# Sliding-window attention and MLP on one core: q and k in DRAM by 48 rows a head, values' halves swapped at the store, addends and divisions placed away from their transfers

## The chip, the cores and the metric

One core of a Trainium2 chip runs the whole program. Its engines each work through their own instructions in order: PE (TensorE, matmuls), PEld (the weight loads of TensorE), DVE (VectorE), ACT (ScalarE), POOL (GpSimd) and SP (SyncE), which here only issues transfers. SBUF is the on-chip working memory, PSUM the memory into which TensorE writes, DRAM the memory outside. The metric is device microseconds of one execution; the profile's span runs from the first to the last instruction of one profiled execution.

## The reference

```python
def _A_ref(x, wqkv, wo):                     # S=2048, D=512, H=32 heads of 16, window W=256
    q, k, v = split(x @ wqkv)
    scores = einsum("bhqd,bhkd->bhqk", q, k) * Dh ** -0.5
    mask = (i - j >= 0) & (i - j < W)
    p = softmax(where(mask, scores, -1e9))
    return merge_heads(einsum("bhqk,bhkd->bhqd", p, v)) @ wo
def _B_ref(x, w1, b1, w2, b2):               # F=1792
    return gelu(x @ w1 + b1) @ w2 + b2
g = sigmoid((x * gate_w).sum(-1, keepdims=True))
return g * A + (1 - g) * B
```

All arrays are float32. The kernel computes a dense product as three matmuls of a rounded high part and a low rest (`mm3`, lines L90 to L92), to keep precision with the narrower matmul type.

## The kernel before

The 2048 tokens are four pieces `t` of 512, and a piece is four blocks of 128. TensorE's work is one long dense program and, woven into it, attention:

- `qkv(t)` transposes x, computes q, k and v, splits q and k into high and low parts (ScalarE L248, VectorE L251) and stores them in DRAM: `SQ`, `SK` (L252), `SV` (L273). The stage lasts some 158 us; attention begins within its last quarter.
- `mlp(n)` runs the two halves of the MLP over the four pieces in eight turns. The end of a block, `y_end` (L647), adds an addend `ya`: the bias `b2` in the first half, the sum of the first half (`YA`) in the second.
- `final(t)` multiplies the attention output with `wo`, scales it by the gate and adds the MLP's part `yb` (L710).

Attention goes over 8 groups of 4 heads, and in each over 16 blocks of 128 keys. `att_max` (matmul L404, VectorE L409) finds row maxima, 8 blocks ahead of `att_exp` (matmul L445, ScalarE L460, GpSimd L451 and L454), which uses them; `att_pv` (L486) multiplies with the values and, by an extra column of ones, gives the denominators. For these, q and k lie in SBUF as 48 rows a head: in `ks` high, low, high, and in `qs` low, high, high, so that one matmul gives the three products. For every group and chunk of 512 tokens, `att_load` and `att_load_v` fetch k, q and v from DRAM. In DRAM a head has 32 rows (high and low), so a tile of 48 takes two loads, one of 32 rows and one of 16; the second head of a pair lies 64 keys displaced in `ks`, and its rows go in two pieces (L365, L367). For the values, the two halves of a block change places (partitions 0 to 63 and 64 to 127) for two of the four heads, at the load (L390, L392).

When a group pair is done for a chunk, `nd` (numerators and denominators) is stored in `ND` (L509). `att_norm` then loads the denominators `den` (L527) and numerators `num` (L530), takes the reciprocal (L533), stores it in `RD` (L534), reads it back spread over 16 rows as `rb` (L535), multiplies (L538) and stores the result in `OT` (L539). `load_o` fetches that as `or` (L567) and splits it into `ot` (L570, L573) for `final`.

The order on PE, ACT, DVE and POOL is written by the program: each function calls `tick` with an assumed duration, and `after(ns, fn)` puts a follow-up that many assumed nanoseconds later (`LAND` 10500, `LANDO` 4500, `NORM` 4500). The order of SP's transfers is made by the scheduling layer from the same program. SP issues them one after another; each waits for its data, for its buffer, and for the transfer eight places earlier in the queue, whose semaphore it uses again. Most of what the change touches is in these lines:

```python
# before, att_norm: what sets the division's place
nc.sync.dma_start(den, v[:, 16, :].rearrange("i (j c) -> i j c", c=32))
nc.sync.dma_start(num, v[:, 0:16, :])
after(NORM, rcp), after(3 * NORM, mul)
# before, mlp, y_start: the addend is loaded when its block's matmuls start
nc.sync.dma_start(ya, b2.partition_broadcast(128))
```

Of the kernel before, what the change touches and what calls it, by code (L numbers as in the profile page):

```python
# [32 lines left out]
def gated_mix(ctx: ExitStack, tc: tile.TileContext, x, wqkv, wo, w1, b1, w2, b2, gate_w, out):  # L33
# [18 lines left out]
    SQ = [dr.tile([H, 16, 2, T], F32, name=f"SQ{t}") for t in range(NT)]  # L52
    SK = [dr.tile([H, 16, 2, T], F32, name=f"SK{t}") for t in range(NT)]
# [180 lines left out]
    def qkv_qk(t, j):  # L234

        xt = xts[t]
        dst, i = (SQ[t], j) if j < NC else (SK[t], j - NC)
# [12 lines left out]
        def lo():  # L250
            nc.vector.tensor_sub(e[:, 1 - h], p, f32(e[:, h]))  # L251
            nc.sync.dma_start(dst[8 * i:8 * i + 8].rearrange("h d s c -> (h d) s c"), f32(e))  # L252
            done.add(("qk", t, j))
        after(100, hi), after(700, lo)

    def qkv_v(t, b):
# [91 lines left out]
    def load_stack(src, high, put):  # L348

        put(0, src.rearrange("h d s c -> (d s) h c"))  # L350
        put(32, src[:, :, high].rearrange("h d c -> d h c"))

    def load_k(g_, c, prs):

        need(("qk", c, NC + g_ // 2))
        for pr in range(prs.start, prs.stop):
            v = f32(ks[:, pr, 2 * c * T:2 * (c + 1) * T])

            def put_a(r, src):
                dst = v[r:r + src.shape[0]].rearrange("r (n x) -> r n x", x=256)[:, :, 64:192]  # L360
                nc.sync.dma_start(dst, src[:, 0].rearrange("r (n x) -> r n x", x=128))

            def put_b(r, src):
                w = v[48 + r:48 + r + src.shape[0]]
                nc.sync.dma_start(w[:, 192:960].rearrange("r (n x) -> r n x", x=256)[:, :, 0:128],  # L365
                                  src[:, 0, 64:448].rearrange("r (n x) -> r n x", x=128))
                nc.sync.dma_start(w.rearrange("r (n x) -> r n x", x=64)[:, 0:16:15],  # L367
                                  src[:, 0].rearrange("r (n x) -> r n x", x=64)[:, 0:8:7])
            for s, put in enumerate((put_a, put_b)):
                h = 4 * g_ + 2 * pr + s  # L370
                load_stack(SK[c][h:h + 1], 0, put)

    def att_load(g_, c, q_only=False):
        need(("qk", c, g_ // 2))
        cs = slice(c * T, (c + 1) * T)
        if not q_only:
            load_k(g_, c, slice(0, 2))
        for s in range(2):
            heads = slice(4 * g_ + s, 4 * g_ + 3 + s, 2)

            def put(r, src):
                nc.sync.dma_start(f32(qs[48 * s + r:48 * s + r + src.shape[0], :, cs]), src)
            load_stack(SQ[c][heads], 1, put)

    def att_load_v(g_, c):
# [4 lines left out]
        nc.sync.dma_start(dst[:, :, 34:68], src[:, :, 68 * g_ + 34:68 * g_ + 68])  # L390
        for r in (0, 64):
            nc.sync.dma_start(dst[64 - r:128 - r, :, 0:34], src[r:r + 64, :, 68 * g_:68 * g_ + 34])  # L392
# [130 lines left out]
    def att_norm(t, c):  # L523
# [4 lines left out]
        num = sb.tile([128, T], F32, tag="tmp", bufs=3, name=f"num{t}_{c}")  # L528
        rb = sb.tile([128, T], F32, tag="tmp", bufs=3, name=f"rb{t}_{c}")
        nc.sync.dma_start(num, v[:, 0:16, :])  # L530

        def rcp():
            nc.vector.reciprocal(den, den)  # L533
            nc.sync.dma_start(RD[t][c].rearrange("h (j c) -> (h j) c", c=32), den)  # L534
            nc.sync.dma_start(rb, RD[t][c].unsqueeze(1).broadcast_to([8, 16, T]))  # L535

        def mul():
            nc.vector.tensor_mul(num, num, rb)  # L538
# [13 lines left out]
    def load_o(t):  # L552

        if t % 2 == 0:
            v = sb.tile([128, NC, 2, T], F32R, tag="xt", bufs=1, name=f"ot{t}")
            ot = [v[:, c] for c in range(NC)]
        else:
            ot = [sb.tile([128, 2, T], F32R, tag="h", bufs=8, name=f"ot{t}_{c}") for c in range(NC)]
        xts["o", t] = ot
        for c in range(NC):  # L560
# [11 lines left out]
            def lo(c=c, raw=raw):  # L572
                nc.vector.tensor_sub(ot[c][:, 1], raw, f32(ot[c][:, 0]))  # L573
                done.add(("ot", t, c))
            land = LAND if t == 0 else LANDO
            after(land + 700 * c, hi), after(land + 700 * c + 600, lo)
# [29 lines left out]

    def mlp(n):
        half, t = TURNS[n]
        last = n % NT == NT - 1
# [20 lines left out]
        ps_, yas = {}, {}  # L630

        def y_start(b):
            if n + 1 == len(TURNS) and b == 2:
                load_o(0)
            ps_[b] = ps.tile([128, D], F32, tag="d", bufs=2, name=f"y{t}_{half}{b}")
            ya = sb.tile([128, D], F32, tag="ya", bufs=2, name=f"ya{t}_{half}{b}")
            if half == 0:
                nc.sync.dma_start(ya, b2.partition_broadcast(128))
            else:
                need(("y", 0, t, b))  # L640
                nc.sync.dma_start(ya, YA[t][slice(b * 128, (b + 1) * 128)])
            yas[b] = ya

        def y_end(b):
            ts = slice(b * 128, (b + 1) * 128)
            y = sb.tile([128, D], F32, tag="sq", bufs=2, name=f"yo{t}_{half}{b}")
            nc.vector.scalar_tensor_tensor(y, ps_[b], 0.5, yas[b], op0=ALU.mult, op1=ALU.add)  # L647
# [172 lines left out]
```

## Time and profile before

| | |
|---|---|
| median of 3 runs | 793.07 us (791.7 to 795.51) |
| the profiled execution | 797.43 us, span 795.7 us |
| granted TensorE clock, mean | 0.987 |
| busy: PE, DVE, ACT, POOL | 760.4, 532.7, 433.1, 386.8 us |
| transfers | 138.74 MB on SP's queue, 57.4% of 16 transfer engines over the span |
| stages by the timeline | projections to 158 us, attention and MLP to about 740, last projection to the end |

In the rows of the profile a group or timeline row names line, engine, instruction, output and inputs with their shapes; a bracket gives the idle time of the engine ahead of it and what ended it. A row of waits gives the total, the number of times and the longest, in us. A row of the windows view gives a stretch, its length, each engine's busy time with its instructions in brackets, and then three numbers: the granted TensorE clock, the busy share of the 16 transfer engines, and GB/s.

### The profile page before, as it was taken

The page shows a single profiled execution, that of the slowest core. Times are in us where ns is not written, and L with a number is a line of the kernel's source. Part 1 is how long each engine was busy: PE and PEld are TensorE (multiplying, and loading weights), DVE is VectorE, ACT ScalarE, POOL GpSimd, SP SyncE. Part 2 cuts the span into 40 slices and gives each one's busy share as a digit, 9 for nine tenths or more (in the row PEclk, how much of TensorE's full clock was granted, in tenths as well). Part 3 has the DMA queues.
Part 4 walks back from the last instruction along what each step waited for, and adds up shares of the span by engine and source line. Part 5 has one row for each costly group of instructions (what it writes and reads, how often), then busy time and mean ns, then how long its engine had stood idle before and what let it go on. Part 6 is the DMA issues. An engine that isn't in the chain of part 4 may idle for free. (4 is left out here: it accounts for less than half of the span.)

```text
span 795.7 us, 18550 instructions
## 1 busy us (share of the span) xinstructions
PE 760.4 (96%) x6102; PEld 629.9 (79%) x6102; DVE 532.7 (67%) x1548; ACT 433.1 (54%) x945; POOL 386.8 (49%) x1125
## 2 busy tenths in 40 slices
PE   8999999989899999999999799999989999999878
PEld 6888888867788878788878677888868788878766
DVE  4433233889579758867996598679757876892433
ACT  4434433466368437745874476458626754875340
POOL 2200000047557755765576467658745775777000
PEclk9999999999999999999999999999989999999999
DMA  9985856536645554755345646534654465546872
GB/s 295 353 301 200 305 176 215 205 106 226 156 113 122 189 161 112 216 141 146 104 116 171 172 137 211 142 86 102 207 155 133 127 206 146 127 143 197 259 258 93
DMA packets 139984, 139.93 MB, mean 176 GB/s; under 512 B 60016, under 2 KB 93040, under 8 KB 139888
## 3 DMA queue, kind: packets, MB, share of 16 engines
q1 hardware_dynamic: 139888, 138.74, 57.4%
q8 instruction: 49, 0.80, 0.5%
q14 instruction: 47, 0.39, 0.2%
HBM read 83.63 MB, written 55.05 MB: 174 GB/s over the span
## 5 line engine op out<-in xcount | busy, mean ns | idle before, releaser
L409 DVE CUSTOM_DVE_ANT_0 jm<-sm,mask 128x384 bf16<-128x384 f32 (+2 forms) x512 | 269.5, 526 | 62.5 <-PE sm L404 34.0
L460 ACT ACTIVATE pt<-st 128x320 f32<-128x320 f32 (+4 forms) x512 | 206.9, 422 | 150.3 <-PE st L445 144.2
L451 POOL TENSOR_SCALAR_AFFINE_SELECT pt<-pt 64x128 f32<-64x128 f32 x512 | 177.3, 346 | 202.5 <-ACT pt L460 182.3
L404 PE MATMUL sm<-ks,qs 96*128 96x384 f32 (+2 forms) x512 | 172.5, 340 | 20.6 <-DVE M L409 19.1
L445 PE MATMUL st<-qs,ks 104*128 104x320 f32 (+4 forms) x512 | 156.3, 307 | 0.7 <-ACT pt L460 0.7
L454 POOL TENSOR_SCALAR_AFFINE_SELECT pt<-pt 64x128 f32<-64x128 f32 x448 | 155.8, 348 | 0.0
L404 PEld LDWEIGHTS sm<-ks,qs 96*128 96x128 f32 x512 | 96.9, 189 | 54.4 <-DVE M L409 32.6
L445 PEld LDWEIGHTS st<-qs,ks 104*128 104x128 f32 x512 | 97.9, 191 | 18.7 <-ACT pt L460 1.1
L90 PE MATMUL y<-w,h 128*128 128x512 f32 x224 | 91.6, 409 | 0.0
L91 PE MATMUL y<-w,h 128*128 128x512 f32 x224 | 88.7, 396 | 0.0
L92 PE MATMUL y<-w,h 128*128 128x512 f32 x224 | 88.3, 394 | 0.0
L429 POOL CAST qs<-tt 8x256 fp32r<-8x256 f32 x128 | 61.5, 481 | 49.7 <-PE u L92 39.1
L90 PE MATMUL u<-mx,w 128*128 128x512 f32 x196 | 81.7, 417 | 0.0
L91 PE MATMUL u<-mx,w 128*128 128x512 f32 x196 | 77.9, 397 | 0.0
L92 PE MATMUL u<-mx,w 128*128 128x512 f32 x196 | 77.6, 396 | 0.0
L486 PE MATMUL pv_st<-pt,vbuf 64*32 64x320 f32 (+4 forms) x1408 | 76.7, 358 | 0.0
L486 PE MATMUL pv_sm<-pt,vbuf 64*32 64x320 f32 (+4 forms) x1408 | 76.2, 358 | 0.5 <-DVE M L409 0.5
L486 PEld LDWEIGHTS pv_st<-pt,vbuf 64*32 64x32 f32 x1408 | 58.4, 109 | 5.8 <-issue 0.9
L486 PEld LDWEIGHTS pv_sm<-pt,vbuf 64*32 64x32 f32 x1408 | 55.9, 109 | 8.7 <-DVE M L409 2.5
L251 DVE TENSOR_TENSOR qke<-qk,qke 128x512 fp32r<-128x512 f32 x32 | 22.1, 690 | 48.9 <-ACT qke L248 40.5
L92 PEld LDWEIGHTS y<-w,h 128*128 128x128 f32 x224 | 42.2, 188 | 10.5
L248 ACT ACTIVATE qke<-qk 128x512 fp32r<-128x512 f32 x32 | 19.1, 598 | 55.9 <-PE qk L92 37.0
(123 smaller groups left out, 1316.9 us busy)
## 6 DMA issues: line engine op xcount, KB each, us to landing
mx<-XT SPq DMA_DIRECT2D x24, 512.0 KB
SQ<-qke SPq DMA_DIRECT2D x16, 512.0 KB
SK<-qke SPq DMA_DIRECT2D x16, 512.0 KB
qs<-SQ SPq DMA_DIRECT2D x64, 128.0 KB
ND<-nd SPq DMA_DIRECT2D x32, 256.0 KB
raw_w<-in_B_w_dram SPq DMA_DIRECT2D x28, 256.0 KB
SV<-vx SPq DMA_DIRECT2D x16, 272.0 KB
xr<-in_A_x_dram SPq DMA_DIRECT2D x16, 256.0 KB
```

The lines of the kernel that those rows point to most:

```text
L90: nc.tensor.matmul(p, lh, rh, start=first, stop=False)
L91: nc.tensor.matmul(p, lh, rl, start=False, stop=False)
L92: nc.tensor.matmul(p, ll, rh, start=False, stop=last)
L251: nc.vector.tensor_sub(e[:, 1 - h], p, f32(e[:, h]))
L404: nc.tensor.matmul(p[:, :w], qs[0:96, pr, b * 128:(b + 1) * 128], of_head(ks[0:96, pr, 2 * k0:2 * (k0 + w)], s), start=True, stop=True)
L409: nc.vector.tensor_tensor_reduce(junk[:, :w], p[:, :w], mask[:, 384 - w:384], 1.0, -3e38, ALU.add, ALU.max, M[:, b % RB, i:i + 1])
L429: nc.gpsimd.tensor_copy(dst, tt[32 * i:32 * i + 8].unsqueeze(1).broadcast_to([8, 2, RB, 32]))
L445: nc.tensor.matmul(p[:, :w], ks[0:104, pr, 2 * k0:2 * k0 + 128], qs[0:104, pr, k0:k0 + w], start=True, stop=True)
L451: nc.gpsimd.affine_select(out=v[:, :, 0:64], in_=v[:, :, 0:64], pattern=[[0, 2], [1, 64]], compare_op=ALU.is_ge, fill=0.0, base=0, channel ...
L454: nc.gpsimd.affine_select(out=v[:, :, W:W + 64], in_=v[:, :, W:W + 64], pattern=[[0, 2], [-1, 64]], compare_op=ALU.is_ge, fill=0.0, base=- ...
L460: nc.scalar.activation(pt[:, pr, :w], p[:, :w], AF.Exp, scale=SCALE)
L486: nc.tensor.matmul(pv[r // 64][32 * i:32 * i + 32, q - c * T:e - c * T], vs(i, r), rhs(r), start=start, stop=last, skip_group_check=True, ...
```

## The change

- `SQ` and `SK` have 48 rows a head. After a q or k tile, two transfers are issued: high and low (two of three rows), and once more the row that occurs twice. A chunk's q is then one load for all four heads, k one load a head. `SK` is one tensor over all tokens, so that the displaced head is loaded across the chunk's border: the last 64 keys of a chunk come with the next chunk's load.
- The values' halves change places when they are stored: three transfers a block instead of one. The load of a chunk is then one transfer.
- `att_norm`: `den` is loaded as before, the reciprocal comes 6000 ns behind (4500 before); `num` and `rb` are requested at 10500 and multiplied at 17000 (13500 before).
- The addend `ya` of a block is loaded when the block two before it has ended (`ya_load`).
- `load_y(0)` goes ahead to the last MLP block, `load_o(t + 1)` ahead of the remaining `load_y`; the last piece's last part is loaded by itself in the third block of `final(2)`. `LANDO` is 5000 instead of 4500.

```diff
-    SQ = [dr.tile([H, 16, 2, T], F32, name=f"SQ{t}") for t in range(NT)]
-    SK = [dr.tile([H, 16, 2, T], F32, name=f"SK{t}") for t in range(NT)]
+    SQ = [dr.tile([H, 48, T], F32, name=f"SQ{t}") for t in range(NT)]
+    SK = dr.tile([H, 48, S], F32, name="SK")
...
-            nc.sync.dma_start(dst[8 * i:8 * i + 8].rearrange("h d s c -> (h d) s c"), f32(e))
+            to = dst[8 * i:8 * i + 8].rearrange("h (d u) c -> (h d) u c", u=3)
+            nc.sync.dma_start(to[:, 0:2], f32(e))
+            nc.sync.dma_start(to[:, 2], f32(e[:, h]))
...
-            nc.sync.dma_start(SV[t][ts], vx)
+            to = SV[t][ts].rearrange("p (g s a) c -> p g s (a c)", s=2, a=2)
+            vy = vx.rearrange("p (g s a) c -> p g s (a c)", s=2, a=2)
+            nc.sync.dma_start(to[:, :, 1], vy[:, :, 1])
+            for r in (0, 64):
+                nc.sync.dma_start(to[64 - r:128 - r, :, 0], vy[r:r + 64, :, 0])
...
-            for s, put in enumerate((put_a, put_b)):
-                h = 4 * g_ + 2 * pr + s
-                load_stack(SK[c][h:h + 1], 0, put)
+            for s in range(2):
+                src = SK[4 * g_ + 2 * pr + s]
+                v = f32(ks[48 * s:48 * s + 48, pr])
+                if s == 0:
+                    w = f32(ks[0:48, pr, 2 * c * T:2 * (c + 1) * T]).rearrange("r (n x) -> r n x", x=256)
+                    nc.sync.dma_start(w[:, :, 64:192], src[:, c * T:(c + 1) * T].rearrange("r (n x) -> r n x", x=128))
+                    continue
+                k0, n = (c * T - 64, NB) if c else (64, NB - 1)
+                w = v[:, 2 * k0 + 64:2 * k0 + 64 + 256 * n].rearrange("r (n x) -> r n x", x=256)
+                nc.sync.dma_start(w[:, :, 0:128], src[:, k0:k0 + 128 * n].rearrange("r (n x) -> r n x", x=128))
...
-        for s in range(2):
-            heads = slice(4 * g_ + s, 4 * g_ + 3 + s, 2)
...
-            load_stack(SQ[c][heads], 1, put)
+        nc.sync.dma_start(f32(qs[0:96, :, c * T:(c + 1) * T]),
+                          SQ[c][4 * g_:4 * g_ + 4].rearrange("(a s) r c -> (s r) a c", a=2))
...
-        nc.sync.dma_start(dst[:, :, 34:68], src[:, :, 68 * g_ + 34:68 * g_ + 68])
-        for r in (0, 64):
-            nc.sync.dma_start(dst[64 - r:128 - r, :, 0:34], src[r:r + 64, :, 68 * g_:68 * g_ + 34])
+        nc.sync.dma_start(dst, src[:, :, 68 * g_:68 * g_ + 68])
...
-        nc.sync.dma_start(num, v[:, 0:16, :])
...
-            nc.sync.dma_start(rb, RD[t][c].unsqueeze(1).broadcast_to([8, 16, T]))
+
+        def back():
+            for name, src in (("num", v[:, 0:16, :]), ("rb", RD[t][c].unsqueeze(1).broadcast_to([8, 16, T]))):
+                tiles.append(sb.tile([128, T], F32, tag="tmp", bufs=3, name=f"{name}{t}_{c}"))
+                nc.sync.dma_start(tiles[-1], src)
...
-        after(NORM, rcp), after(3 * NORM, mul)
+        after(6000, rcp), after(10500, back), after(17000, mul)
...
+    def ya_load(k):
+        n, b = divmod(k, NB)
+        if n == len(TURNS):
+            return
+        half, t = TURNS[n]
+        yas[k] = ya = sb.tile([128, D], F32, tag="ya", bufs=2, name=f"ya{t}_{half}{b}")
+        if half == 0:
+            nc.sync.dma_start(ya, b2.partition_broadcast(128))
+        else:
+            need(("y", 0, t, b))
+            nc.sync.dma_start(ya, YA[t][slice(b * 128, (b + 1) * 128)])
...
-            nc.vector.scalar_tensor_tensor(y, ps_[b], 0.5, yas[b], op0=ALU.mult, op1=ALU.add)
+            nc.vector.scalar_tensor_tensor(y, ps_[b], 0.5, yas.pop(n * NB + b), op0=ALU.mult, op1=ALU.add)
+            ya_load(n * NB + b + 2)
...
+            if n + 1 == len(TURNS) and b == 3:
+                load_y(0)
...
-        if t == 0:
-            for i in (0, 1, 2):
-                load_y(i)
-        if t == 1:
-            load_y(3)
         if t < NT - 1:
-            load_o(t + 1)
+            load_o(t + 1, range(NC) if t < NT - 2 else range(NC - 1))
+        for i in ((1, 2), (3,), (), ())[t]:
+            load_y(i)
...
+            if t == NT - 2 and b == 2:
+                load_o(t + 1, range(NC - 1, NC))
...
-LANDO = 4500.0
+LANDO = 5000.0
```

PE's and POOL's instructions stand in the same order as before. Three places show what moves on the others.

On SP, in the middle of attention, from the store of the third chunk's `nd` of the second group pair to the load of its denominators (`raw_w` are MLP weights, `OT` a finished division, `YA` a sum of the first MLP half). Before:

```order
L509 DMA ND_1_99<-nd_2_6192 128x512
L365 DMA ks<-SK_76 32x3x128
L367 DMA ks<-SK_76 32x2x64
...
L382 DMA qs<-SQ_72 16x2x512
L390 DMA vbuf<-SV_81 128x4x34
L392 DMA vbuf<-SV_81 64x4x34 x2
L137 DMA raw_w_6245<-in_B_w_dram 128x512
L539 DMA OT_87<-num_1_6003 128x512
L648 DMA YA_124<-yo_03_6260 128x512
L527 DMA den_1_6293<-ND_1_99 128x1x32
```

Now, for the same chunk:

```order
L364 DMA ks<-SK 48x4x128
L378 DMA qs<-SQ_72 96x2x512
L531 DMA rb_1_6035<-RD_1_108 128x1x512
L386 DMA vbuf<-SV_78 128x4x68
L503 DMA ND_1_96<-nd_2_6045 128x512
L521 DMA den_1_6133<-ND_1_96 128x1x32
L618 DMA ya_11_6100<-YA_121 128x512
```

The loads of k, q and values that stood between the store and the denominators' load are fewer and stand ahead of the store. Over the program SP issues 655 transfers where it issued 975.

On DVE, the reciprocal of the same denominators among the row maxima (`jm`, two rows each). Before:

```order
L149 TENSOR_TENSOR w_8_6349<-raw_w_6157,w_8_6349 128x512
L533 RECIPROCAL den_1_6293<-den_1_6293 128x32
L409 ISA jm_7_0_6371,M_4_6103<-sm_7_0_6369,mask 128x384
L409 ISA M_4_6103 128x1
L409 ISA jm_7_3_6376,M_4_6103<-sm_7_3_6374,mask 128x384
```

Now:

```order
L149 TENSOR_TENSOR w_8_6188<-raw_w_6006,w_8_6188 128x512
L403 ISA jm_7_0_6207,M_4_5952<-sm_7_0_6205,mask 128x384
L403 ISA M_4_5952 128x1
L403 ISA jm_7_3_6212,M_4_5952<-sm_7_3_6210,mask 128x384
L403 ISA M_4_5952 128x1
L403 ISA jm_7_2_6229,M_4_5952<-sm_7_2_6227,mask 128x384
L403 ISA M_4_5952 128x1
L525 RECIPROCAL den_1_6133<-den_1_6133 128x32
```

It stands three maxima later.

On SP, at the end of the projections, around the last k tile's store (`SK<-qke_7`). Before:

```order
L365 DMA ks<-SK_76 16x3x128
L252 DMA SK_77<-qke_7_1429 128x1024
L367 DMA ks<-SK_76 16x2x64
L382 DMA qs<-SQ_72 32x2x512
L382 DMA qs<-SQ_72 16x2x512
```

Now:

```order
L615 DMA ya_00_1470<-in_B_b_dram 128x512
L615 DMA ya_01_1472<-in_B_b_dram 128x512
L253 DMA SK<-qke_7_1469 128x2x512
L254 DMA SK<-qke_7_1469 128x512
L364 DMA ks<-SK 48x4x128
L368 DMA ks<-SK 48x4x128
L364 DMA ks<-SK 48x4x128
L368 DMA ks<-SK 48x4x128
L378 DMA qs<-SQ_72 96x2x512
```

The third chunk's k (keys 960 to 1471 for the displaced heads) is loaded behind that store; before, its loads were spread ahead of it.

More of the change, by code (lines that the diff above doesn't have):

```diff
@@ L356, in load_k @@
         for pr in range(prs.start, prs.stop):
[L357 to L368, printed above, removed]
@@ L527, in att_norm @@
         nc.sync.dma_start(den, v[:, 16, :].rearrange("i (j c) -> i j c", c=32))
-        num = sb.tile([128, T], F32, tag="tmp", bufs=3, name=f"num{t}_{c}")
-        rb = sb.tile([128, T], F32, tag="tmp", bufs=3, name=f"rb{t}_{c}")
-        nc.sync.dma_start(num, v[:, 0:16, :])
+        tiles = []
         def rcp():
@@ L550, in load_x, with load_o @@
         xts[t] = xt
[L552 to L560, printed above, removed]
+    def load_o(t, cs=range(NC)):
+        if ("o", t) not in xts:
+            if t % 2 == 0:
+                v = sb.tile([128, NC, 2, T], F32R, tag="xt", bufs=1, name=f"ot{t}")
+                xts["o", t] = [v[:, c] for c in range(NC)]
+            else:
+                xts["o", t] = [sb.tile([128, 2, T], F32R, tag="h", bufs=8, name=f"ot{t}_{c}") for c in range(NC)]
+        ot = xts["o", t]
+        for c in cs:
             need(("o", t, c))
@@ L574, in lo @@
                 done.add(("ot", t, c))
+            n = cs.index(c)
             land = LAND if t == 0 else LANDO
-            after(land + 700 * c, hi), after(land + 700 * c + 600, lo)
+            after(land + 700 * n, hi), after(land + 700 * n + 600, lo)
     TURNS = [(0, 3), (0, 0), (0, 1), (0, 2), (1, 2), (1, 0), (1, 1), (1, 3)]
```

26 lines of the change are left out of this document (11 added, 15 removed).

## The prediction

> **What bounds the kernel now.** I read the busy times first, then the waits of TensorE, then its idle gaps one by one in the timeline, and for each gap the row of VectorE that ended it.
>
> ```profile
> PE 760.4 (96%) x6102; PEld 629.9 (79%) x6102; DVE 532.7 (67%) x1548; ACT 433.1 (54%) x945; POOL 386.8 (49%) x1125
> PE sm L404 <- DVE M L409: 19.1, 20, 4.4
> PE a L90 <- DVE ao L710: 6.7, 3, 2.9
> ```
>
> TensorE is busy 760.4 of 795.7 us, so about 35 us of idle time is all that a change off TensorE can win directly, plus what a lowered clock costs. The second and third rows say who ends that idle time: VectorE, 19.1 us under the row-maximum matmuls (`sm`) and 6.7 us under the last projection (`a`). VectorE is only 67% busy, so it is late by waiting, not by work. Seven gaps carry most of it; the number in brackets is the idle time ahead of the row.
>
> ```profile
> 206.29 0.33 PE L404 MATMUL sm<-ks,qs 96*128 96x128 f32 x1 [2.26 <-DVE M L409]
> 292.90 0.44 PE L404 MATMUL sm<-ks,qs 96*128 96x384 f32 x1 [1.26 <-DVE M L409]
> 456.42 0.69 PE L404 MATMUL sm<-ks,qs 96*128 96x384 f32 x1 [4.40 <-DVE M L409]
> 584.55 0.69 PE L404 MATMUL sm<-ks,qs 96*128 96x384 f32 x1 [2.82 <-DVE M L409]
> 752.71 0.47 PE L90 MATMUL a<-wo,ot 128*128 128x512 f32 x1 [2.18 <-DVE ao L710]
> 762.76 0.50 PE L90 MATMUL a<-wo,ot 128*128 128x512 f32 x1 [1.64 <-DVE ao L710]
> 768.68 0.76 PE L90 MATMUL a<-wo,ot 128*128 128x512 f32 x1 [2.90 <-DVE ao L710]
> ```
>
> Just ahead of the first four, VectorE stood in front of an instruction whose transfer had not landed:
>
> ```profile
> 205.07 0.69 DVE L647 SCALAR_TENSOR_TENSOR yo<-y,ya 128x512 f32<-128x512 f32 x1 [3.60 <-DMA ya<-in_B_b_dram]
> 292.07 0.35 DVE L533 RECIPROCAL den<-den 128x32 f32<-128x32 f32 x1 [3.77 <-DMA den<-ND]
> 455.59 0.35 DVE L533 RECIPROCAL den<-den 128x32 f32<-128x32 f32 x1 [4.90 <-DMA den<-ND]
> 583.73 0.35 DVE L533 RECIPROCAL den<-den 128x32 f32<-128x32 f32 x1 [4.19 <-DMA den<-ND]
> ```
>
> One of them is the MLP addend `ya`, three are the softmax denominators `den`. VectorE works in order, so the maxima behind them wait, their three PSUM buffers stay full, and TensorE stops. A stop also costs something after it has ended. The windows view from the restart on gives the granted clock (third number from the end):
>
> ```profile
> 206.29:212.00 5.71, 5.71 (x113) 4.80 (x114) 2.83 (x14) 1.91 (x4) 2.77 (x9) 1.00 0.46 121
> 292.90:298.00 5.10, 4.97 (x100) 3.51 (x100) 3.45 (x12) 0.88 (x2) 2.65 (x8) 0.67 0.45 133
> 456.42:462.00 5.58, 5.58 (x56) 4.52 (x63) 5.21 (x17) 2.71 (x6) 2.10 (x5) 0.57 0.46 125
> 584.55:592.00 7.45, 7.45 (x106) 5.70 (x107) 3.35 (x12) 1.33 (x3) 2.69 (x8) 0.57 0.66 199
> 768.68:773.00 4.32, 4.32 (x13) 3.45 (x14) 0.52 (x1) 1.73 (x4) 0.00 (x0) 0.64 0.92 302
> ```
>
> TensorE works there at a reduced clock: lost are 0.33 x 5.10 = 1.7, 0.43 x 5.58 = 2.4, 0.43 x 7.45 = 3.2 and 0.36 x 4.32 = 1.6 us; after the gap at 206 nothing. The Trainium skill ("TensorE: Matmul & The Clock Gate", section "What's actually happening") lets the clock fall only after an idle window of about 3.4 us. This trace differs: it fell after 1.26 us and stayed up after 2.26 us. By the page only the gap of 4.40 us would pay, and the sum below would be smaller by 1.7 + 3.2 + 1.6 = 6.5 us.
>
> **Why `den` is late.** The queue of SyncE, which issues every transfer in order, around the worst case:
>
> ```profile
> 442.88 0.34 SPq L509 DMA_DIRECT2D ND<-nd  x1
> ...
> 445.16 3.30 SPq L382 DMA_DIRECT2D qs<-SQ  x4
> 448.56 0.38 SPq L390 DMA_DIRECT2D vbuf<-SV  x1
> 448.99 1.29 SPq L392 DMA_DIRECT2D vbuf<-SV  x2
> ...
> 451.92 0.62 SPq L527 DMA_DIRECT2D den<-ND  x1
> ```
>
> The store of `nd` goes out at 442.88, the load of its denominators at 451.92: nine microseconds of k, q and value loads lie between. The division was placed by the planner's clock, not by that queue.
>
> **The change, part by part.**
>
> *Attention loads.* A chunk and group issued 12 loads of k, 4 of q and 3 of values; now 4, 1 and 1 (two or four short k pieces more at the first and last chunk). At 0.38 to 0.82 us each (1.29/2, 3.30/4 in the fence above), 13 fewer give SyncE, at 0.45, some 6 us of each chunk's 18. The queue order shows the result: the `den` load stands directly behind the `nd` store, where it can go out as soon as the store has landed. The `den` division is moved later by 1.5 us (6000 for 4500 ns), the reload of numerators and reciprocals and the multiply by 3.5. Both sides move away from each other: about 9 us of queue removed, 1.5 added, against a wait of 4.9 at most. I take the three `den` stops as gone: 1.26 + 4.40 + 2.82 + 1.7 + 2.4 + 3.2 = 15.8 us.
>
> *MLP addend.* `ya` is now loaded two blocks ahead, when its buffer comes free, instead of when its matmuls start. The wait of 3.60 us goes: 2.26 us on TensorE. Together 18.0. TensorE will not run gapless there: its other gaps ahead of `sm` are about 0.5 us each with no transfer behind them, so I leave 0.5 for each of the four and take **16** (bounds 0, if another wait takes their place, and 18).
>
> *Last tokens.* The three gaps and the clock are 2.18 + 1.64 + 2.90 + 1.6 = 8.3 us. VectorE stood behind the split of the attention output, whose load was late:
>
> ```profile
> 760.69 1.19 ACT L570 ACTIVATE ot<-or 128x512 fp32r<-128x512 f32 x2 [8.28 <-DMA or<-OT]
> 761.35 0.69 DVE L573 TENSOR_TENSOR ot<-or,ot 128x512 fp32r<-128x512 f32 x1 [4.78 <-ACT ot L570]
> ```
>
> Now the first MLP sums are fetched before the last MLP block, the outputs of the next tokens ahead of the remaining sums, and the last piece, which is waited for longest, alone at the third block. Against it: its division is finished 3.5 us later. A final step is 4 blocks of 12 matmuls at 0.227 us, 10.9 us, so two steps lie between the last multiply and its use; 3.5 us fit. I take **6** of 8.3 (bounds 0 and 8.3).
>
> *Projections, where the price is.* q and k are stored with 48 rows a head instead of 32, by one more transfer each, and each value store becomes three, in pieces of 2 x 17 floats, 136 bytes.
>
> ```profile
> SQ<-qke SPq DMA_DIRECT2D x16, 512.0 KB
> SK<-qke SPq DMA_DIRECT2D x16, 512.0 KB
> SV<-vx SPq DMA_DIRECT2D x16, 272.0 KB
> 0.00:158.00 158.00, 155.54 (x709) 126.95 (x710) 68.46 (x164) 62.88 (x126) 13.30 (x41) 1.00 0.74 257
> 20.00:28.00 8.00, 8.00 (x39) 6.63 (x38) 5.10 (x11) 4.56 (x10) 3.06 (x2) 1.00 1.03 414
> ```
>
> The last two rows give the transfer engines' share (0.74) and rate over the projections, and the rate when they are full (414 GB/s). They work 0.74 x 158 = 117 us. The extra rows are 32 x 256 KB = 8.4 MB, at 414 GB/s 20 us. The values are 16 x 2048 packets of 136 bytes. No row shows such a store; the nearest is that of the reciprocals, 128 packets of 128 bytes, alone on the engines:
>
> ```profile
> 709.01 0.33 SPq L534 DMA_DIRECT2D RD<-den  x1
> 709.80:710.20 0.40, 0.40 (x4) 0.34 (x3) 0.40 (x2) 0.14 (x1) 0.40 (x2) 1.00 0.27 41
> 450.30:452.30 2.00, 1.71 (x8) 1.09 (x7) 0.39 (x1) 1.54 (x4) 1.34 (x4) 1.00 0.61 55
> ```
>
> 0.27 x 0.40 x 16 engines over 128 packets is 13.5 ns. The value loads of now, 136 bytes read, bound it from above: 55 GB/s x 2 us = 110 KB or 809 packets in 0.61 x 2 x 16 = 19.5 us, 24 ns. I take 13.5, the same direction: 16 x 2048 x 13.5 / 16 = 28 us instead of 4.5 MB / 414 = 11. The stage then holds 117 + 20 + 17 = 154 us of transfers in 158. It is nearly full, so loads queue behind stores, but TensorE waits for none as long as it fits. It fits up to 15.5 ns a packet; each further ns is 2.05 us of lateness, at 24 ns 17 us.
>
> Who would notice first: the last 64 keys of a chunk now come with the next chunk's load. Block 7 needs keys of chunk 2, whose load stands in the queue behind the store of the last k tile.
>
> ```profile
> 150.99 0.34 SPq L252 DMA_DIRECT2D SK<-qke  x1
> 159.08 0.34 PE L404 MATMUL sm<-ks,qs 96*128 96x384 f32 x1
> ```
>
> From 150.99 four loads and two stores are issued by about 154; block 7 starts at 159.08. Some 2 us are spare. In the steady part the same keys are issued 13 us ahead of use, so there it costs nothing. I charge **1.5** for this stage (bounds 0 and 18, the lateness at 24 ns; all of it would be TensorE's).
>
> Sum against the profiled execution: 797.43 - 16 - 6 + 1.5 = 776.9. It lies 4.4 above the median, 793.07; since such stops come and go between executions but the work behind them does not, I take the sum as the median of the changed kernel: **777 us**.
>
> **Rivals.**
>
> *B, the projections run late.* 16 to 24 ns a packet: 1 to 17 us of lateness less the 2 spare. At 20 ns: 4.5 x 2.05 - 2 = 7, with some 3 us of reduced clock after such a stop and without the 1.5 charged, 777 + 7 + 3 - 1.5 = 786. For it: 24 ns in the reads. Against: 13.5 in the only store.
>
> *C, slower.* The same place, at 27 ns, twice the measured store: 11.5 x 2.05 - 2 = 22, and 3 of clock, 777 + 25 - 1.5 = 800. It turns from gain to loss at about 25 ns. The Trainium skill ("DMA: Bandwidth & Descriptors", section "Specifications") says that below 512 bytes the engines read, modify and write, which speaks for this case; no row here shows unaligned pieces stored.
>
> *D, another wait takes the place.* The division of a chunk still waits for two trips through DRAM, and SyncE now stands in front of the `den` load until the store has landed. If half the attention gain and half of the last tokens' are lost: 777 + 8 + 3 = 788.
>
> **How the numbers follow.** The forecast 0.60, B 0.18, C 0.10, D 0.12. About 0.5%, 4 us, is what a measurement can tell from no change: faster is below 789.1, slower above 797. Faster: 0.60 + 0.12 of B + 0.05 of D = 0.77; same 0.06 + 0.07 = 0.13; slower 0.10. Low end: every gap gone, 797.43 - 26.3 = 771, and 1 us below; high end 792, which takes in D and most of B. The forecast's own range is 771 to 784.
>
> **What would show it.** Right: no VectorE wait for `den` or `ya` over 1 us; TensorE's clock at 1.00 over the attention; idle time under `a` below 2 us; transfer share over the first 158 us near 0.97. Wrong: idle time of TensorE between 40 and 165 us, ahead of the transposes of x or of `sm` at block 7, ended by a transfer; value stores above 20 ns a packet; `sm` gaps of the old length with another releaser.

## The result, and the profile after

The changed kernel takes 816.14 us in the median of 4 runs (815.31 to 819.51), beside 793.43 for the kernel before: a ratio of 1.029 (95% interval 1.025 to 1.033). It is slower; 777 was forecast. The profiled execution has a span of 817.8 us, 22.1 more than the 795.7 of before. The runs of every kernel below agree within 1.3%, but for one of 1469.18 us, of the kernel with the values as before, which is left out.

First, where the time lies. The tile view of the first MLP matmuls (`u`) gives the start of the first and of the last one, and that of the last projection (`a`) the start of the last stage. Before, and now:

```profile
L90 PE MATMUL u<-xt,w x28: 389/395/500, 149.2 to 180.5; 128*128 128x512 f32 x28
L92 PE MATMUL u<-mx,w x196: 389/393/628, 221.3 to 706.2; 128*128 128x512 f32 x196
L90 PE MATMUL a<-wo,ot x68: 277/389/763, 739.3 to 791.8; 128*128 128x512 f32 x60, 128*128 128x256 f32 x8
```

```profile
L90 PE MATMUL u<-xt,w x28: 389/395/628, 189.2 to 220.5; 128*128 128x512 f32 x28
L92 PE MATMUL u<-mx,w x196: 389/393/399, 258.8 to 730.1; 128*128 128x512 f32 x196
L90 PE MATMUL a<-wo,ot x68: 277/389/765, 763.3 to 814.1; 128*128 128x512 f32 x60, 128*128 128x256 f32 x8
```

The three marks move from 149.2, 706.2 and 739.3 to 189.2, 730.1 and 763.3. TensorE's order is the same in both, so the marks can be compared: the projections end 40.0 us later; from there to the last `u` 540.9 us pass instead of 557.0, so 16.1 are won in the attention; and from the first `a` to the end it is 54.5 instead of 56.4. 40.0 - 16.1 - 1.9 is 22.0: nearly the whole difference. The forecast for the attention was 16. The error lies in the projections alone, where 1.5 was charged.

TensorE's waits, and its gaps over 1.6 us, in the timeline of the changed kernel:

```profile
PE xp L204 <- DMA xr<-in_A_x_dram: 12.8, 3, 6.4
PE sm L398 <- DVE M L403: 9.4, 16, 1.7
...
64.06 1.11 PE L204 MATMUL xp<-ident,xr 128*128 128x128 f32 x4 [6.22 <-DMA xr<-in_A_x_dram]
107.13 1.11 PE L204 MATMUL xp<-ident,xr 128*128 128x128 f32 x4 [6.36 <-DMA xr<-in_A_x_dram]
153.77 0.79 PE L90 MATMUL qk<-xt,qk 128*128 128x512 f32 x1 [6.60 <-ACT vx L273]
160.18 0.30 PE L398 MATMUL sm<-ks,qs 96*128 96x128 f32 x1 [1.91 <-DMA qs<-SQ]
169.20 0.39 PE L398 MATMUL sm<-ks,qs 96*128 96x256 f32 x1 [1.66 <-DVE M L403]
180.69 0.79 PE L90 MATMUL qk<-xt,qk 128*128 128x512 f32 x1 [5.30 <-DVE qke L251]
789.97 0.77 PE L90 MATMUL a<-wo,ot 128*128 128x512 f32 x1 [4.62 <-DVE ao L720]
```

The three long stops for `den` are gone: ahead of `sm` only two stops exceed 1.3 us, both still in the projections. Instead there are six stops between 64 and 181 us, 28 us together; the first two wait for the load of x. At 153.77 and 180.69 it is a load as well: ScalarE, and VectorE through it, stood in front of a weight that had not landed.

```profile
152.54 0.63 ACT L145 ACTIVATE w<-raw_w 128x512 fp32r<-128x512 f32 x1 [10.06 <-DMA raw_w<-in_B_w_dram]
178.68 0.63 ACT L145 ACTIVATE w<-raw_w 128x512 fp32r<-128x512 f32 x1 [9.99 <-DMA raw_w<-in_B_w_dram]
```

In the queue of SyncE the loads stand behind the value stores. The first load of x for the next tokens, before, and now with a store ahead of it:

```profile
41.30 0.33 SPq L189 DMA_DIRECT2D xr<-in_A_x_dram  x1
```

```profile
46.42 4.11 SPq L278 DMA_DIRECT2D SV<-vx  x1
...
54.78 2.28 SPq L189 DMA_DIRECT2D xr<-in_A_x_dram  x4
```

It goes out at 54.78 instead of 41.30. The four blocks of values hold SyncE from 36.0 to 54.7 us. The pieces move in four bursts, one for each 512 tokens. How fast they move shows in stretches that hold little else: the transfer view from 42 to 53 us, in the first burst, and from 86 to 100 us, in the second. Short packets are those under 512 bytes; the row of the queue (`q1`) ends with the busy share of the 16 engines.

```profile
DMA packets 5499, 0.52 MB, mean 48 GB/s; under 512 B 5494, under 2 KB 5494, under 8 KB 5498
q1 hardware_dynamic: 5498, 0.51, 45.8%
```

```profile
DMA packets 6030, 0.80 MB, mean 57 GB/s; under 512 B 6030, under 2 KB 6030, under 8 KB 6030
q1 hardware_dynamic: 6030, 0.80, 138.0%
```

The first stretch misleads. Its packets have 94 bytes in the mean, not 136, because the load of the bias `b1c` (L320, issued at 45.68 us) falls into it: 7.0 KB, fetched as 1792 single numbers of 4 bytes. The "about 500 packets a microsecond" of the expectations below is 5494 / 11, with these counted in. The second stretch holds almost only value pieces: 6030 in 14 us are 431 a microsecond, so 16 / 0.431 = 37 ns of each engine's time for one. The busy share says something else each time: 0.458 x 11 x 16 / 5499 = 14.7 ns a packet in the first stretch, 1.38 x 14 x 16 / 6030 = 51 ns in the second.

The stops cost again after they end. The windows view with the granted clock (third number from the end):

```profile
60.00:80.00 20.00, 15.94 (x68) 13.21 (x69) 4.04 (x6) 6.47 (x12) 0.62 (x4) 0.83 1.04 371
100.00:120.00 20.00, 13.64 (x54) 10.89 (x53) 3.59 (x6) 5.91 (x10) 0.46 (x3) 0.83 1.06 300
140.00:160.00 20.00, 11.68 (x44) 8.88 (x42) 1.38 (x2) 3.50 (x9) 0.15 (x1) 0.83 1.31 178
160.00:180.00 20.00, 13.56 (x47) 10.41 (x47) 5.30 (x21) 2.43 (x5) 0.00 (x0) 0.77 1.06 95
180.00:200.00 20.00, 19.31 (x80) 16.09 (x80) 17.59 (x54) 7.45 (x13) 1.58 (x4) 0.89 1.01 344
```

Busy time times the missing share is 0.17 x (15.94 + 13.64 + 11.68) + 0.23 x 13.56 + 0.11 x 19.31 = 12.3 us. With the 28 of idle time that makes 40.

### The profile page after: what moved, and what is told of

Its sections match the earlier page's. It is cut to its first block, busy times and chain, and to the rows that moved or that the text cites. A ratio compares the mean times of both kernels' runs of the same rounds, so it can differ in the third digit from the quotient of the medians.

```text
span 817.8 us, 18283 instructions
## 1 busy us (share of the span) xinstructions
PE 766.9 (94%) x6102; PEld 636.1 (78%) x6102; DVE 533.5 (65%) x1548; ACT 433.3 (53%) x945; POOL 384.3 (47%) x1125
## 4 chain that ended last, share of the span: by engine, by line
PE 73%; DMA 10%; DVE 8%; issue 4%; SPq 3%; ACT 2%; DVEq 0%; ACTq 0%
PE sm L398 9%; PE st L439 7%; PE y L90 7%; PE y L91 6%; PE y L92 6%; PE u L90 5%; PE pv_st L480 5%; PE u L91 4%; PE u L92 4%; DVE jm L403 4%; PE pv_sm L480 4%; DMA xr<-in_A_x_dram 3%; PE qk L90 3%; PE qk L92 3%; PE qk L91 3%
## 5 line engine op out<-in xcount | busy, mean ns | idle before, releaser
L480 PE MATMUL pv_st<-pt,vbuf 64*32 64x320 f32 (+4 forms) x1408 | 73.5, 347 | 0.0
L480 PE MATMUL pv_sm<-pt,vbuf 64*32 64x320 f32 (+4 forms) x1408 | 73.0, 346 | 0.0
L480 PEld LDWEIGHTS pv_st<-pt,vbuf 64*32 64x32 f32 x1408 | 56.5, 106 | 4.7
L480 PEld LDWEIGHTS pv_sm<-pt,vbuf 64*32 64x32 f32 x1408 | 53.8, 106 | 7.5 <-issue 2.4
L251 DVE TENSOR_TENSOR qke<-qk,qke 128x512 fp32r<-128x512 f32 x32 | 22.1, 690 | 52.6 <-ACT qke L248 42.6
L268 POOL MEMSET vx<- 128x32 f32 x16 | 2.4, 155 | 110.0 <-DMA SQ<-qke 77.6
```

What stands on the lines that cost most here:

```text
L480: nc.tensor.matmul(pv[r // 64][32 * i:32 * i + 32, q - c * T:e - c * T], vs(i, r), rhs(r), start=start, stop=last, skip_group_check=True, ...
```

## Experiments: which part it is

Theory S: the small value stores alone hold up the projections, and the rest of the forecast holds. Q: the extra rows of q and k share the blame. Ratios below are to the kernel before, measured on the same chip beside each kernel.

**Values as before, all else changed.**

```diff
-            nc.sync.dma_start(to[:, :, 1], vy[:, :, 1])
-            for r in (0, 64):
-                nc.sync.dma_start(to[64 - r:128 - r, :, 0], vy[r:r + 64, :, 0])
+            nc.sync.dma_start(SV[t][ts], vx)
...
-        nc.sync.dma_start(dst, src[:, :, 68 * g_:68 * g_ + 68])
+        nc.sync.dma_start(dst[:, :, 34:68], src[:, :, 68 * g_ + 34:68 * g_ + 68])
+        for r in (0, 64):
+            nc.sync.dma_start(dst[64 - r:128 - r, :, 0:34], src[r:r + 64, :, 68 * g_:68 * g_ + 34])
```

> The changed kernel with the values stored and loaded as before (one store a block in whole rows, the halves swapped by three loads); q and k keep their 48 rows, division, addends and last tokens their new places. Theory S (the stores in pieces of 136 bytes alone hold up the projections: 16 x 2048 pieces at about 500 a microsecond are 65 us of SyncE's queue): the first row maximum returns from 160 to about 132.5 us, the 40 us go, 816 - 40 + about 2 = 776 to 781. Rival Q (the 8.4 MB and 32 stores more of q and k share the blame in a stage that is full): about half comes back, 795 to 800. Rival I (the chunk's last 64 keys come too late, whatever the stores): TensorE still stands at block 7, over 785.

Measured: 778.94 us in the median of three runs, ratio 0.975 (0.971 to 0.980). The loss is gone, and the gain that was forecast is there. Q falls.

**Halves of a row in one piece.** The heads stand ordered by half, so that a store moves 256 pieces of 1088 bytes a block and still swaps the halves.

```diff
-    SV = [dr.tile([T, H, 17], F32, name=f"SV{t}") for t in range(NT)]
+    SV = [dr.tile([128, 2 * NB, H * 17 // 2], F32, name=f"SV{t}") for t in range(NT)]
...
-            to = vx[:, :, 0:16].rearrange("p (g s a) d -> p g a s d", s=2, a=2)
+            to = vx[:, :, 0:16].rearrange("p (s g a) d -> p g a s d", s=2, a=2)
...
+            vy = vx.rearrange("p (s x) c -> p s (x c)", s=2)
+            nc.sync.dma_start(SV[t][:, 2 * b + 1], vy[:, 1])
+            for r in (0, 64):
+                nc.sync.dma_start(SV[t][64 - r:128 - r, 2 * b], vy[r:r + 64, 0])
...
+        nc.sync.dma_start(dst, SV[c][:, :, 34 * g_:34 * g_ + 34])
```

> The changed kernel with the halves still swapped at the store, but heads ordered so that each half of a row is one piece of 1088 bytes in SBUF and in DRAM: 256 pieces a block in place of 2048; the load is still one, in pieces of 136 bytes. Theory S: 16 x 256 pieces cost some 8 us of the queue at most, so as fast as with the values' old way or a little faster, 775 to 780. If swapping at the store costs by itself (three stores and the wait on their landing, whatever their pieces), it stays above 800. Rival Q: 795 to 800.

Measured: 779.39 us, ratio 0.976 (0.971 to 0.980), the first `u` at 148.9 us. As many stores, as many waits, the same bytes: it is the pieces, not the swap at the store.

**The swap alone, and the 48 rows alone,** each put into the kernel before.

> The kernel before with the values' swap at the store alone (pieces of 136 bytes), nothing else. Theory S: transfers of the first 158 us grow from 117 to 117 - 11 + 65 = 171, 13 us late, less 2 spare and with 3 of lowered clock: 793 + 14 = 807 (800 to 813). Theory Q or an interplay of both stores: under 797, since 171 overshoots by little and only both together overfill the stage.

> The kernel before with q and k in 48 rows alone (two stores a tile, one load a chunk and head, the chunk's last 64 keys with the next chunk); division, addends and values as before. Theory S: 20 us more of transfers fit (137 of 158), so no loss there; the relief of SyncE by some 11 loads a chunk is worth part of the 16 us of the attention: 778 to 790. Theory Q: the projections end late, 797 to 810. Rival I: block 7 waits for its keys, TensorE idle there over 3 us.

Measured: the swap alone 807.93 us, ratio 1.011 (1.004 to 1.017); the 48 rows alone 777.47 us, ratio 0.974 (0.971 to 0.978). With the swap alone the first `u` starts at 174.7 us, 25.5 late, and the attention gives 11.5 of that back. The difference, 14 us, is the loss that was expected (the medians differ by 9), but by luck: the lateness was put too low, and the gain was not foreseen. The 48 rows alone end the projections at 148.6, and no wait for keys shows:

```profile
0.00:158.00 158.00, 155.12 (x711) 126.78 (x712) 68.91 (x165) 62.89 (x127) 13.40 (x41) 1.00 0.90 313
...
DVE den L524 <- DMA den<-ND: 0.3, 1, 0.3
L90 PE MATMUL u<-xt,w x28: 389/395/628, 148.6 to 180.0; 128*128 128x512 f32 x28
L92 PE MATMUL u<-mx,w x196: 389/393/400, 218.6 to 688.7; 128*128 128x512 f32 x196
```

The transfers' share rises from 0.74 to 0.90 and fits, and the attention takes 540.1 us with the division at its old place. The 48 rows alone win what all of the change wins there. In SyncE's timelines the mechanism shows: for the divisions behind the three stops for `den`, 5.7, 9.0 and 8.6 us passed between the store of `nd` and the issue of the load of `den`; with the 48 rows alone it is 5.4, 3.2 and 3.9. The middle one:

```profile
436.38 0.43 SPq L500 DMA_DIRECT2D ND<-nd  x1
...
439.60 0.61 SPq L518 DMA_DIRECT2D den<-ND  x1
```

**The new places alone** (division, addends, last tokens), with q, k and values as before.

> The kernel before with the new places of division, addends and last tokens alone; q, k and values stored and loaded as before. Theory S as it stands after the four runs: the queue of SyncE is what made the denominators late, so the new places alone win the addend's stop and at most half of the rest: ratio 0.985 to 0.997. Rival (the places are what cleared the stops, the fewer loads only came along): ratio 0.975 to 0.98, as with the 48 rows alone.

Measured: 787.82 us, ratio 0.987 (0.983 to 0.992). The attention takes 548.5 us, 8.6 less than before; the denominators still come late:

```profile
DVE den L532 <- DMA den<-ND: 10.5, 5, 4.2
PE sm L405 <- DVE M L410: 10.8, 17, 2.4
```

In the queue nothing is relieved: the same three loads go out 7.5, 9.7 and 7.8 us behind their stores. So the two gains in the attention overlap: 16.9 us by the rows alone, 8.6 by the places alone, 16.1 by both.

## Experiments: what a small store costs, and why

**Twice the pieces, the same bytes.** Every piece of 136 bytes goes as two of 68.

```diff
-            nc.sync.dma_start(to[:, :, 1], vy[:, :, 1])
-            for r in (0, 64):
-                nc.sync.dma_start(to[64 - r:128 - r, :, 0], vy[r:r + 64, :, 0])
+            for a in range(2):
+                nc.sync.dma_start(to[:, :, 1, a], vy[:, :, 1, a])
+                for r in (0, 64):
+                    nc.sync.dma_start(to[64 - r:128 - r, :, 0, a], vy[r:r + 64, :, 0, a])
```

> The changed kernel with every piece of 136 bytes stored as two of 68 bytes: the same bytes, 4096 pieces a block, six stores a block. If the price is by the piece (500 a microsecond), 65 us more of the queue: 870 to 885. If it is by the byte, or by the wait for each store to land, not by pieces: 816 to 830.

Measured: 880.39 us, ratio 1.104 (1.099 to 1.109). By the two ratios that is some 60 us more for 32768 pieces more, 1.8 ns each. In the second burst, from 104 to 128 us:

```profile
DMA packets 11319, 0.75 MB, mean 31 GB/s; under 512 B 11319, under 2 KB 11319, under 8 KB 11319
q1 hardware_dynamic: 11319, 0.75, 139.7%
```

472 packets a microsecond, against 431 of twice the size. So the price is nearly by the piece. A busy share over 100% can only be packets counted side by side, so it can't give this price.

**Two issuing queues.** ScalarE issues the two half stores, SyncE the other.

```diff
-                nc.sync.dma_start(to[64 - r:128 - r, :, 0], vy[r:r + 64, :, 0])
+                nc.scalar.dma_start(to[64 - r:128 - r, :, 0], vy[r:r + 64, :, 0])
```

> The changed kernel with the two half stores of each value block (1024 of 2048 pieces) issued by ScalarE instead of SyncE. If one issuing queue takes small pieces at 500 a microsecond and the 16 engines could take more, the blocks go twice as fast (about 1000 packets a microsecond in the first value stage at 36 to 55 us, which ends by about 46), and the 40 us of lateness fall to 15 or less: under 792. If the engines themselves take no more than about 500 a microsecond, that rate stays, and the time stays over 800 unless the loads, in a queue of their own, pass the stores by; then the packet rate tells, not the time.

Measured: 816.62 us, ratio 1.024 (1.020 to 1.029). The transfer view from 85 to 94 us, in the second burst, and the queues and ScalarE's work in the first:

```profile
DMA packets 4068, 0.71 MB, mean 79 GB/s; under 512 B 3626, under 2 KB 4068, under 8 KB 4068
...
39.15 5.33 SPq L278 DMA_DIRECT2D SV<-vx  x1
44.52 1.71 SPq L189 DMA_DIRECT2D xr<-in_A_x_dram  x2
...
49.28 0.52 ACTq L280 DMA_DIRECT2D SV<-vx  x1
49.92 0.66 ACT L273 ACTIVATE vx<-v 128x256 f32<-128x256 f32 x2 [5.76 <-DMA SV<-vx]
```

3626 short packets in 9 us are 403 a microsecond, with 0.2 MB of other transfers beside them. So a second issuing queue doesn't raise the rate; what limits it lies behind the queues. The Trainium skill ("DMA: Bandwidth & Descriptors", section "Queues, rings and completion order") states that both queues feed the same 16 engines. The trace agrees with that: 403 from two queues, 431 from one. Whether the engines or the memory behind them set the rate, no run shows. The first load of x now passes stores by and goes out at 44.52 us, ten microseconds sooner, and yet the first `u` starts at 185.5, 36.3 late. The stores hold up more than the queue: ScalarE waits 5.76 us until the buffer of a store is free again.

**A slot of 512 bytes for every piece.** As many pieces of 136 bytes, none sharing an aligned stretch of 512 bytes with another.

```diff
-    SV = [dr.tile([T, H, 17], F32, name=f"SV{t}") for t in range(NT)]
+    SV = [dr.tile([T, H // 2, 128], F32, name=f"SV{t}") for t in range(NT)]
...
+            to = SV[t][ts].rearrange("p (g s) c -> p g s c", s=2)
+            nc.sync.dma_start(to[:, :, 1, 0:34], vy[:, :, 1])
+            for r in (0, 64):
+                nc.sync.dma_start(to[64 - r:128 - r, :, 0, 0:34], vy[r:r + 64, :, 0])
```

> The changed kernel with every piece of 136 bytes stored in a slot of its own of 512 bytes in DRAM, so that no two pieces lie in one aligned stretch of 512 bytes; as many pieces, two loads instead of one. If the price of a store comes from neighbours that share such a stretch, the rate rises from about 500 packets a microsecond towards the 920 that loads of such pieces reached, and the 40 us of lateness fall to some 10: 780 to 790. If every short piece written costs the same wherever it lies, the rate stays and so does the time: 812 to 822.

Measured: 787.95 us, ratio 0.990 (0.987 to 0.993). Number and size of the pieces are those of the changed kernel; only where they lie is new, and that a chunk's values take two loads. Two more runs tell sharing from the place at which a piece begins.

**The same slots, begun 20 bytes later; and slots 192 bytes apart.** The loads follow the stores.

```diff
-            nc.sync.dma_start(to[:, :, 1, 0:34], vy[:, :, 1])
+            nc.sync.dma_start(to[:, :, 1, 5:39], vy[:, :, 1])
```

```diff
-    SV = [dr.tile([T, H // 2, 128], F32, name=f"SV{t}") for t in range(NT)]
+    SV = [dr.tile([T, H // 2, 48], F32, name=f"SV{t}") for t in range(NT)]
```

> As the slots of 512 bytes, but each piece begins 20 bytes into its slot: still no two pieces in one stretch of 512 bytes, but no piece begins at a multiple of 32 or 64 bytes. If the slow stores of the changed kernel come from neighbours in one stretch, this stays as fast as the slots that begin at 0: ratio 0.985 to 0.995, the value stage at about 750 packets a microsecond. If they come from beginnings off a multiple of 64 bytes, it falls back to the changed kernel's: ratio 1.02 to 1.03 and about 500.

> As the slots of 512 bytes, but the slots are 192 bytes apart: every piece begins at a multiple of 64 bytes and shares no 64 bytes with a neighbour, while two or three pieces lie in one stretch of 512 bytes. If sharing 512 bytes is what makes the stores slow, ratio 1.02 to 1.03 and about 500 packets a microsecond. If only sharing (or half writing) a smaller line does, ratio 0.985 to 0.995 and about 750.

Measured: begun at 20 bytes 840.4 us, ratio 1.054 (1.047 to 1.061); 192 bytes apart 792.52 us, ratio 0.998 (0.995 to 1.001). The transfer views of the second burst: slots at 0 (78.5 to 86 us), slots at 20 bytes (93 to 107), slots 192 bytes apart (78.5 to 88), and the swap alone (78 to 87):

```profile
DMA packets 5889, 0.78 MB, mean 105 GB/s; under 512 B 5889, under 2 KB 5889, under 8 KB 5889
```

```profile
DMA packets 5154, 0.69 MB, mean 49 GB/s; under 512 B 5154, under 2 KB 5154, under 8 KB 5154
```

```profile
DMA packets 6466, 0.86 MB, mean 91 GB/s; under 512 B 6465, under 2 KB 6465, under 8 KB 6466
```

```profile
DMA packets 3862, 0.57 MB, mean 63 GB/s; under 512 B 3831, under 2 KB 3833, under 8 KB 3862
```

The first three are 785, 368 and 681 packets a microsecond. The same pieces in slots of the same size move at less than half the rate when they begin at 20 bytes. Pieces that begin at a multiple of 64 bytes are fast whether they share a stretch of 512 bytes or not; the difference between 785 and 681, and between 787.95 and 792.52 us, is small beside it and stays open. In the changed kernel a piece begins at a multiple of 136, so one in eight begins at a multiple of 64: an estimate from the two rates, 1 / (0.125 / 785 + 0.875 / 368) = 395, lies near its 431. So the beginning decides, not the neighbours. Whether 32 bytes would do, and whether what counts is how many stretches of 64 bytes a piece fills only in part, was not tried.

Lateness of the first `u` against the kernel before, with the estimate of the prediction's own sum (transfers of the stage less 158 us, less 2 spare) at each measured rate:

| kernel | short packets a us, second burst | by the sum | measured |
|---|---|---|---|
| changed | 431 | 117 + 20 - 11 + 76 - 160 = 42 | 40.0 |
| pieces of 68 bytes | 472 | 105 | 99.6 |
| slots of 512 bytes | 785 | 8 | 10.2 |
| slots 192 bytes apart | 681 | 14 | 14.7 |
| slots begun at 20 bytes | 368 | 55 | 63.2 |
| swap alone | 426 | 117 - 11 + 77 - 160 = 23 | 25.5 |

All six agree within some 8 us. The prediction's sum holds with the measured rate in it; its 117 is still a busy share times a length, of a stage of mostly large transfers.

**A version that beats both.** Halves of 1088 bytes and 48 rows, first with the division back at its old places, then with the multiply at 15500 instead of 13500.

```diff
-        after(6000, rcp), after(10500, back), after(17000, mul)
+        after(NORM, rcp), after(3 * NORM, mul)
```

> The changed kernel with the values in halves of 1088 bytes and the division at its old places (reciprocal at 4500, multiply at 13500, the numerators loaded at once); addends and last tokens as changed. If the later division is what made the last tokens' one stop of 5.8 us, it goes: 772 to 776, with a ratio of 0.968 to 0.972. If the later division is needed in the attention, stops of 1 to 4 us ahead of the row maxima come back: 780 to 790.

```diff
-        after(NORM, rcp), after(3 * NORM, mul)
+        after(NORM, rcp), after(15500, mul)
```

> The kernel with halves of 1088 bytes, 48 rows, reciprocal and reloads at their old places, and the multiply at 15500 for 13500, so that in the last tokens it stands behind the output addition for which TensorE's PSUM waits, instead of ahead of it. If the multiply's wait for its reciprocals (1.4 us, and 0.7 of work) was part of the stop of 4.3 us, some 2 us go: ratio 0.970 to 0.973. If the splits of the next outputs ahead of it set the stop, nothing changes: 0.974.

Measured: 776.33 us, ratio 0.974 (0.971 to 0.977), and 773.05 us, ratio 0.972 (0.968 to 0.976). The intervals overlap, so the last step is not shown by the times; the traces show what it does. VectorE ahead of the stop of the last tokens, with the multiply at 13500, and at 15500 with TensorE's row:

```profile
741.63 2.00 DVE L566 TENSOR_TENSOR ot<-or,ot 128x512 fp32r<-128x512 f32 x3 [0.71 <-ACT ot L563]
745.02 0.69 DVE L530 TENSOR_TENSOR num<-num,rb 128x512 f32<-128x512 f32 x1 [1.40 <-DMA rb<-RD]
745.63 1.40 DVE L715 SCALAR_TENSOR_TENSOR ao<-a,g,yb 128x512 f32<-128x512 f32 x2
```

```profile
743.77 0.69 DVE L566 TENSOR_TENSOR ot<-or,ot 128x512 fp32r<-128x512 f32 x1 [0.75 <-ACT ot L563]
744.38 0.74 DVE L715 SCALAR_TENSOR_TENSOR ao<-a,g,yb 128x512 f32<-128x512 f32 x1
745.36 0.69 DVE L530 TENSOR_TENSOR num<-num,rb 128x512 f32<-128x512 f32 x1 [0.24 <-DVE ao L715]
...
745.26 0.47 PE L90 MATMUL a<-wo,ot 128*128 128x512 f32 x1 [3.15 <-DVE ao L715]
```

The multiply no longer stands ahead of the output addition (`ao`) that frees TensorE's PSUM, and the stop falls from 4.3 to 3.2 us, about half of what was expected. What still stands ahead of it are the splits of the next outputs. Nor do the times show either kernel to be faster than the 48 rows alone (0.971 to 0.978): the swap at the store, even in long pieces, adds nothing to them that was measured.

The three stages, from the tile views and the span of one execution of each kernel:

| kernel | first `u` | first to last `u` | first `a` to the end |
|---|---|---|---|
| before | 149.2 | 557.0 | 56.4 |
| changed | 189.2 | 540.9 | 54.5 |
| halves of 1088 bytes | 148.9 | 540.1 | 55.7 |
| 48 rows alone | 148.6 | 540.1 | 53.5 |
| swap alone | 174.7 | 545.5 | 55.3 |
| new places alone | 149.4 | 548.5 | 55.6 |
| old division | 148.7 | 537.9 | 54.5 |
| multiply at 15500 | 148.9 | 537.2 | 52.9 |

## Why the prediction was wrong

- **The step that failed: the price of a value store, "I take 13.5, the same direction".** It was worked out as busy share times length over packets, from one store of 128 packets. From one packet to the next an engine needs 37 ns where stores are queued behind one another, and the 28 us of the sum were 32768 / 431 = 76. The busy share can't give this price: in the two stretches above it makes 14.7 and 51 ns of the same stores. And the 128 packets, at a share of 0.27, did not fill the engines; their pieces of 128 bytes lie one behind the other, so each begins at a multiple of 64 bytes, which most of those of 136 do not.
- **The bound of 24 ns was misread.** The view of that window of value loads counts 610 packets, not 809, since the 110 KB hold larger ones:

```profile
DMA packets 610, 0.11 MB, mean 55 GB/s; under 512 B 593, under 2 KB 593, under 8 KB 610
```

  By the same reckoning that is 32 ns. That it lies near 37 is luck, for these are loads, with gaps between them.
- **Rival C was the case,** at the place that it named, and had a chance of 0.10 because its price was put at 27 ns. At 37 its sum gives 21.5 x 2.05 - 2 = 42 us and 777 + 42 + 3 - 1.5 = 821, against 816. The 3 us for the clock came on top there; the measured 40 hold 12 us of lowered clock already. By this sum the turn from gain to loss lies at 23.5 ns, not at 25. The page of the Trainium skill that spoke for it ("DMA: Bandwidth & Descriptors", section "Specifications") names 512 bytes as the least for full rate, with read, modify and write below. Here pieces of 136 bytes, all below 512, differ by a factor of two with the place where they begin (785 against 368); what the engines do with a short piece no run shows.
- **"The first 158 us are nearly full, but fit"** was the right reckoning with a wrong term: with the measured rates the same sum gives the lateness of six kernels within some 8 us.
- **Who would notice first** was said to be `sm` at block 7, for its keys. It was the transposes of x, at 64 us, which the prediction named among what would prove it wrong. With the 48 rows alone the keys are in time.
- **Attention, 16:** right, 16.1. So was that SyncE's queue made `den` late: the 48 rows alone win 16.9. VectorE waits for `den` once over 1 us, 1.3, and never for `ya`. The later division was not needed for it: with halves of 1088 bytes the stage is no longer with the division at its old place (537.9 against 540.1, one execution each). That the new places alone would win the addend's stop and at most half of the rest was right too: 8.6.
- **Last tokens, 6:** wrong. 56.4 became 54.5 us. Three stops became one of 4.62, behind splits whose loads were late. The new order adds nothing to what the relieved queue gives: the 48 rows alone, with the old order, take 53.5 us; rows, halves of 1088 bytes and new order 55.7 (one execution each, and the values' loads differ too, so the order is not shown alone). Something of rival D is there: a stop of the same place with another length.
- **Transfer share near 0.97** as a sign was useless: it was 1.06 over 158 us in a stage that ran 40 us late, and 0.46 from 42 to 53 us, while the stores held SyncE.

## What to carry to other kernels

Price a transfer in small pieces by the time that passes from packet to packet in a stretch where the queue is backed up, never by the engines' busy share. When data must be rearranged on its way through DRAM, order it so that each store moves long pieces, or at least pieces that begin at a multiple of 64 bytes: with long pieces alone the changed kernel went from a loss of 2.9% to a gain of 2.4%, with begins at multiples of 64 bytes to a gain of 1.0%. Count in a stretch only what belongs to it: its packets may be those of another transfer. And a change of several parts has to be taken apart: here one part, the 48 rows, wins 2.6% alone, as much as all parts together without the short stores, and these lose twice as much beside them.

## What the runs showed of the hardware that was not expected

- Stores of 136 bytes to DRAM: 785 a microsecond over the 16 engines when each begins at a multiple of 64 bytes in a slot of 512, 681 in slots of 192; 431 when one in eight begins so; 368 when all begin 20 bytes behind. Pieces of 68 bytes: 472. Two issuing queues don't raise it (403, with other transfers beside).
- Loads of 136-byte pieces don't show that. In the kernel with halves of 1088 bytes all pieces of one load begin at the same place in a stretch of 64 bytes: in the first load (group 0) at a multiple of 64, in the fifth (group 1) 8 bytes behind one. Both pass over 900 short packets in 1.0 us, from 172.7 and from 241.1 us on:

```profile
DMA packets 977, 0.25 MB, mean 253 GB/s; under 512 B 920, under 2 KB 920, under 8 KB 977
```

```profile
DMA packets 946, 0.13 MB, mean 127 GB/s; under 512 B 946, under 2 KB 946, under 8 KB 946
```

- The busy share of the engines was 0.46 at 499 short packets a microsecond (42 to 53 us) and 1.38 at 431 (86 to 100 us).
- After each stop of 5.3 to 6.6 us TensorE's clock was lower for a time, 0.77 to 0.89 over windows of 20 us.
